# Rounds 3 to 7 of a recurrence kernel: w, k and r loaded in runs of steps and turned by VectorE in 32x32 squares

## The chip, the core and the metric

The kernel runs on one core of a Trainium2 chip. The core has five instruction streams that run side by side and wait for each other through semaphores: PE (TensorE, matrix products, which take their weights through a separate load, PEld), DVE (VectorE), ACT (ScalarE), POOL (GpSimd) and SP (SyncE, which here only issues DMAs). PE writes to PSUM, from where DVE or ACT copy results to SBUF. The metric is device time in microseconds (us) of one execution of the whole program, the median of three runs.

## What is computed

A recurrence over 768 steps for 4 batches and 8 heads of 48 columns, then a layer norm and a two-layer MLP with a residual, on rows of 8 x 48 = 384 columns. All in 32-bit floats.

```python
# r, k, v, w: (4, 8, 768, 48); u: (8, 48)
for t in range(S):
    kt, vt, rt, wt = (k[:, :, t], v[:, :, t], r[:, :, t], w[:, :, t])
    cur = np.einsum('bhd,bhe->bhde', u[None] * kt, vt)
    y[:, :, t] = np.einsum('bhd,bhde->bhe', rt, state + cur)
    state = wt[:, :, :, None] * state + np.einsum('bhd,bhe->bhde', kt, vt)
...
x = y as (4, 768, 384)
mu, var = mean and variance of x over its 384 columns
xn = (x - mu) / np.sqrt(var + 1e-06) * g_ln
out = x + np.maximum(xn @ w_ch1, 0.0) @ w_ch2     # 384 -> 1536 -> 384
```

## The kernel before

**Rounds and units.** The 4 x 768 steps are cut into 8 rounds of 384 steps, each of two units of four heads. Even rounds begin a batch. Round r's recurrence runs while the MLP of the round before fills PE's time; the loop variable `rnd` counts the round whose recurrence is on.

**The recurrence by levels.** Steps are handled in chunks of 64. The decay between two steps is built up by doubling, in six levels (`NLEV`): on level `lev`, `quads` multiplies, for all chunks of a unit, the r of the right half of each block of 2 x 2^lev steps with the k of its left half (`a_ps`, 96 small products for a round and level in the profile), `grow` then multiplies r and k by the decays (`tot`, products of w made by `totals`) so that they fit the next level (`rkT`, two instructions on DVE), and `keep` copies the right places of the products into the chunk matrix A (a copy under a mask on DVE). So each level is a chain: PE, DVE, PE. `ends`, `states`, `exchanged`, `own_outputs` and `outputs` carry the state from chunk to chunk and make the outputs (`kn_ps`, `kv`, `s`, `sx`, `y`, `x`).

**Turned inputs.** `quads` wants w, k and r with the head column on the partitions and the steps along the row. Two heads stand in the two halves of the 128 partitions (a pair, `pr`). Before the change `load` brings `nat[nm]`, 128 steps by heads of 64 columns of which 48 are filled, in three DMAs a tensor and unit (rows of 192 bytes), one round ahead; `turned` turns one pair of one unit with three TensorE transposes of 128x128 into a PSUM tile of the pool `ps_t` (two buffers), and ACT copies it to `rkT` or `wT`. Three tensors, two units and two pairs make 12 such calls, 36 transposes, in a round. `own_products` also reads the natural k and r, for the term of a step with itself (`rk`, `own`, `vo`).

**What fills PE.** `mlp` is a generator of 24 steps: 12 that make one 128-row part of the hidden layer each (`h_ps`, copied through ReLU by ACT), and 12 that add up outputs (`o_ps`, to which DVE adds x). Each step is three 32-bit products of 384 columns, which the profile shows as six matmuls. `fill(until, tasks)` spreads a level's list of tasks evenly among the MLP steps due by then (`UNTIL`). In level 3 the statistics and `norm` of the finished round make `xn` on DVE; in level 4 `turned_x` turns `xn` on PE (`xT_ps`) for the next MLP.

**Which level turns what.** With `first = 3` in `rnd` 2 and `first = 1` after that, level `first` turns w of both units of the next round, the next level k and r of its first unit, the one after that k and r of its second unit.

**Order.** PE, ACT, DVE and POOL, and DMAs issued through `SPO`, are held to the order of the program. DMAs issued through `SP` are placed in the queue by a scheduler; once placed, the queue is in order too. The tag `raw` has four buffers; before the change only the MLP's weights pass through them, in `rnd` 0 and 1.

**The start.** Round 0's w, k and r come in whole rows by `load_rows`, from SP and from ACT. ACT loads its function table for a first square root (`root`). `warm` issues products of a zero tile (`nought`, "idle" in the profile).

Of the kernel before, what the change touches and what calls it, by code (L numbers as in the profile page):

```python
# [9 lines left out]
F32 = mybir.dt.float32  # L10
# [4 lines left out]
AF = mybir.ActivationFunctionType  # L15
# [37 lines left out]
def kernel(  # L53
# [16 lines left out]
    SP = nc.sync  # L70

    B, H, S, D = r.shape
    P = 128
# [59 lines left out]
    def load_rows(nm, q, eng):  # L133

        b, f, g = units[q]
        src = {"w": w, "k": k, "r": r}[nm]
        eng.dma_start(
            out=flat(nm, q)[:, 0 : NH * TT * D].rearrange("p (h x) -> p h x", h=NH),
            in_=src[b, ts(g, NH), ds(f * RN, RN)].rearrange("h (p c) d -> p h (c d)", c=TT),
        )  # L140

    def load_v(q, eng=SP):
        vn[q] = p4.tile([P, TT, NH, D], F32, tag="v", name=f"v{q}")
        for c in range(TT):
            eng.dma_start(out=vn[q][:, c], in_=steps(v, q, c))
# [9 lines left out]
            )  # L155


    nought = const.tile([P, 1], F32, name="nought")
    DVE.memset(nought, 0.0)
    eps = const.tile([P, 1], F32, name="eps")  # L160
    DVE.memset(eps, 1e-6)
    load_rows("r", 0, ACT)

    ACT.activation(out=const.tile([P, 1], F32, name="root"), in_=eps, func=AF.Sqrt)
    for q in range(U):
        load_rows("w", q, SPO)
        load_rows("k", q, SPO)
    load_rows("r", 1, ACT)

    sel = const.tile([P, H // 2, 2], F32, name="sel")  # L170
    POOL.memset(sel, 0.0)
    for j in range(2):
        ACT.dma_start(
            out=sel[ds(HP * j, D), :, j], in_=u.rearrange("(r j) d -> j d r", j=2)[j]
        )
    g_sb = const.tile([P, KC], F32, name="g_sb")
    u_bc = const.tile([P, H, D], F32, name="u_bc")
    ident = const.tile([P, P], F32, name="ident")
    make_identity(nc, ident)
    for q in range(U):  # L180
        for nm in "wrk":
            POOL.memset(flat(nm, q)[:, NH * TT * D :], 0.0)
# [109 lines left out]
    def warm(n, tag="m"):  # L292

        while n > 0:
            m = min(n, RN // P)
            ps = (ps_m if tag == "m" else ps_t).tile([P, RN], F32, tag=tag, name="idle")
            PE.matmul(
                ps[:, 0 : m * P], nought.broadcast_to([P, P]), nought.broadcast_to([P, m * P]),
                start=True, stop=True,
            )  # L300
            n -= m


    st, carry = {}, {}

    def turned(q, nm, pr):
        a = st.setdefault(q, {})
        if pr == 0:
            if nm == "w":
                if q % U == 0:  # L310
                    st["w"] = p1.tile([P, U, W], F32, tag="w", name=f"wT{q // U}")
                a["w"] = st["w"][:, q % U]
            elif "rk" not in a:

                rk = a["rk"] = p4.tile([P, 2, W], F32, tag="rkT", name=f"rkT{q}")
                a["r"], a["k"] = rk[:, 0], rk[:, 1]
        ps = ps_t.tile([P, RN], F32, tag="t", name=f"{nm}_ps{q}_{pr}")
        if q < U:


            for c in range(TT):
                for j in (1, 0):
                    at = ((2 * pr + j) * TT + c) * D - HP * j
                    PE.transpose(
                        ps[0 : HP * (j + 1), ts(c, P)],
                        flat(nm, q)[:, ds(at, HP * (j + 1))], ident,
                    )
            (DVE.tensor_copy if q == 0 and pr else ACT.copy)(
                out=a[nm][:, ts(pr, RN)].rearrange("p (m c) -> p m c", c=TT),
                in_=ps.rearrange("p (c m) -> p m c", c=TT),  # L330
            )
            return
        for c in range(TT):
            PE.transpose(
                ps[:, ts(c, P)],
                nat[nm][q % 2][:, c, ts(pr, 2)].rearrange("p j d -> p (j d)"), ident,
            )
        ACT.copy(out=a[nm][:, ts(pr, RN)], in_=ps)
# [46 lines left out]
    def product_sums(q):  # L385
        b, f, g = units[q]
        a = st[q]
        ps = ps_t.tile([P, RN], F32, tag="t", name=f"own_ps{q}")
        for pr in pairs:
            for c in range(TT):  # L390
                PE.matmul(
                    ps[:, ts(pr * TT + c, 2)], a["ruk"][pr][:, ts(c, P)],
                    sel[:, NP * g + pr], start=True, stop=True,
                )
        o = a["own"] = p4.tile([P, TT, NH], F32, tag="own", name=f"own{q}")
        ACT.copy(
            out=o.rearrange("p c (r j) -> p r c j", j=2),
            in_=ps[:, 0 : 2 * NK].rearrange("p (r c j) -> p r c j", r=NP, j=2),
        )
# [145 lines left out]
    def own_outputs(q, tag="a"):  # L545

        y = ys[q] = banks(tag, f"y{q}")
        A = a_bufs[q // U % 2]
        for k_ in range(NK):
            pr, c = divmod(k_, TT)  # L550
            for i in range(2):
                for j in range(2):
                    rows = ds(C * (i ^ j), C)
                    PE.matmul(
                        y[j][ds(C * i, C), k_], A[rows, j, q % U, k_, :],
                        vx[q][rows, c, pr] if j else vn[q][rows, c, 2 * pr],
                        start=k_ == 0, stop=False, skip_group_check=True,
                    )

    def outputs(q):  # L560
        b, f, g = units[q]
        if q not in ys:
            own_outputs(q)
        a, y = st.pop(q), ys.pop(q)
        if g == 0:
            xs[b, f] = p2.tile([P, TT, H, D], F32, tag="x", name=f"x{b}_{f}")

        for k_ in range(NK):
            pr, c = divmod(k_, TT)
            for i in range(2):  # L570
                for j in range(2):
                    rows = ds(HP * (i ^ j), D)
                    if i:
                        R, s = a["rx"][rows, k_], a["sx"][rows, pr, c]
                    elif c:
                        R, s = a["r"][rows, ts(2 * k_, C)], a["s"][rows, pr, 2 * c - 1]
                    elif a["before"] is not None:
                        R, s = a["r"][rows, ts(2 * k_, C)], a["before"][rows, pr, 2 * TT - 1]
                    else:
                        continue  # L580
                    PE.matmul(
                        y[j][ds(C * i, C), k_], R, s,
                        start=False, stop=True, skip_group_check=True,
                    )
        for j in range(2):
            DVE.tensor_tensor(
                out=xs[b, f][:, :, ts(g, NH)]
                .rearrange("p c (r j) e -> p j r c e", j=2)[:, j],
                in0=y[j].rearrange("p (r c) e -> p r c e", r=NP),
                in1=a["vo"].rearrange("p c (r j) e -> p j r c e", j=2)[:, j], op=ALU.add,  # L590
            )
        del vn[q], vx[q]
# [117 lines left out]
    def each(f, *ranges):  # L710
        calls = [()]
        for r_ in ranges:
            calls = [c + (x,) for c in calls for x in r_]
        return [lambda c=c: f(*c) for c in calls]
# [37 lines left out]
    begin()  # L752
    begin()
    load(new[1], "k", SPO)
    SPO.dma_start(out=g_sb, in_=moe_g_ln.rearrange("(kc p) -> p kc", p=P))
    warm(3)
    grow(u1, 0)
    keep(0, 0)
    ahead = each(turned, new[:1], "wrk", pairs) + each(turned, new[1:], "wrk", pairs)
    for lev in range(1, NLEV):  # L760
        quads(u0, lev)
        if lev == 1:
            product_sums(u0)
        quads(u1, lev)
        run(ahead[2 * lev - 2 : 2 * lev] if lev < NLEV - 1 else [])
        if lev in (2, 3, 4):
            begin()
        if lev < NLEV - 1:
            warm(3)
        for which in ("rk",) if lev < NLEV - 1 else "kr":  # L770
            for q in (u0, u1):
                grow(q, lev, which)
        keep(0, lev)
# [13 lines left out]
    product_sums(u1)  # L787
    own_term(u1, POOL)
    own_outputs(u0)
    outputs(u0)  # L790
    exchanged(u1)
    begin()
    shifted()
    own_outputs(u1, "m")
    warm(2, "t")
    outputs(u1)
    moments(0)
    load(units_of(2)[0], "w", SPO)
# [23 lines left out]
    for rnd in range(1, NR + 1):  # L822
# [3 lines left out]
        for lev in range(NLEV):  # L826
# [37 lines left out]
                if lev in (4, 5):  # L864
                    own_term(now[lev - 4], POOL)
            if rnd == 2 and lev == 0:
                tasks += each(load_v, now) + each(load, new, "w")
            if rnd == 2 and lev == 2:
                for q in now:
                    take(DVE, q)  # L870
                    tasks += each(load, new[q % U :][:1], "kr")
            if rnd == 2 and lev in (3, 4):
                tasks += each(own_term, now[lev - 3 :][:1], [POOL])
            if rnd > 2 and lev < 2:
                tasks += each(load, new, ["w", "kr"][lev])
            first = 3 if rnd == 2 else 1
            if rnd > 1 and new and first <= lev < first + 3:
                m = lev - first
                tasks += each(turned, new[m - 1 : m], "kr", pairs) if m else each(
                    turned, new, "w", pairs  # L880
                )
            if rnd == 2:
                if lev == 0:
                    tasks += each(exchanged, old)
# [78 lines left out]
```

## Time and profile before

| | |
|---|---|
| median of three runs | 586.68 us (586.47 to 587.8) |
| the profiled execution | 586.47 us |
| its span, first to last instruction | 584.7 us |
| mean granted TensorE clock | 0.991 |
| `o_ps` matmuls | 576, 199.1 us busy |
| `h_ps` matmuls | 576, 198.9 us busy |
| `a_ps` matmuls | 4608, 78.7 us busy |
| `w_ps`, `k_ps`, `r_ps` transposes | 108 each, 273 ns at the median for one |
| ACT copies of these | 31 each, 0.48 us at the median |
| bytes moved | 36.52 MB, 62 GB/s over the span |
| `nat_w`, `nat_k`, `nat_r` loads | 42 each of 96 KB, 3.2, 3.0 and 2.8 us from issue to landing |

Busy time counts a stretch once where instructions of a group overlap. Matmuls are pipelined, so the length of one is more than what it adds to the end. An arrow in the views names what a wait ended on.

### The profile page before, as it was taken

What the parts mean: (1) busy time and instruction counts of PE and PEld (TensorE: products, weight loads), DVE (VectorE), ACT (ScalarE), POOL (GpSimd) and SP (SyncE); (2) the same over time, 40 slices, a digit from 0 to 9 for tenths busy, and PEclk for the clock granted to TensorE, in tenths of its full rate; (3) what the DMA queues carried; (4) which work ended last, traced back from release to release, by engine and by line L of the source; (5) the groups of instructions that cost most, each with busy time, mean ns of one, the idle gap of its engine ahead of it and who ended that gap; (6) DMA issues with size and microseconds to landing.
All of it is one profiled execution on the core that took longest, in us unless ns stands there. A gap on an engine that the chain in (4) does not pass through costs nothing.

```text
span 584.7 us, 19058 instructions
## 1 busy us (share of the span) xinstructions
PE 571.7 (98%) x8560; PEld 383.3 (66%) x8560; DVE 273.5 (47%) x576; ACT 193.9 (33%) x423; POOL 91.5 (16%) x124
## 2 busy tenths in 40 slices
PE   9999989999999999999999999999999999999997
PEld 6776755666666666666666666667666666666554
DVE  5869899677264634343462543336254531130000
ACT  3657686402442124211432114312331015202200
POOL 7140011104340026000620008000320000000000
PEclk9979899999999999999999999999999999999999
DMA  9937885037314311340205302021000000000000
GB/s 232 212 91 142 198 240 129 9 84 137 61 25 97 77 30 28 63 95 16 57 3 93 65 29 43 2 61 31 15 2 2 16 28 2 2 15 27 0 15 27
DMA packets 114192, 36.52 MB, mean 62 GB/s; under 512 B 104768, under 2 KB 111040, under 8 KB 114112
## 3 DMA queue, kind: packets, MB, share of 16 engines
q1 hardware_dynamic: 112640, 34.72, 26.7%
q8 instruction: 67, 1.10, 0.8%
q10 hardware_dynamic: 1472, 0.59, 0.4%
q14 instruction: 13, 0.11, 0.1%
HBM read 28.51 MB, written 4.72 MB: 57 GB/s over the span
## 4 chain that ended last, share of the span: by engine, by line
PE 91%; ACT 4%; DVE 2%; issue 1%; POOL 1%; DVEq 0%; ACTq 0%; POOLq 0%
PE o_ps L49 32%; PE h_ps L49 30%; PE a_ps L49 11%; PE y L49 4%; PE kv L49 2%; PE k_ps L49 2%; PE w_ps L49 2%; PE kn_ps L49 2%; PE r_ps L49 2%; PE xT_ps L49 1%; ACT rest L49 1%; PE idle L49 1%; PE own_ps L49 1%; ACT rkT L49 1%; DVE w_sb L49 1%
## 5 line engine op out<-in xcount | busy, mean ns | idle before, releaser
L49 PE MATMUL o_ps<-w_sb,h 128*128 128x384 f32 x576 | 199.1, 490 | 0.8 <-ACT h L49 0.8
L49 PE MATMUL h_ps<-xT,w_sb 128*128 128x384 f32 x576 | 198.9, 493 | 0.0
L49 PEld LDWEIGHTS h_ps<-xT,w_sb 128*128 128x128 f32 x576 | 105.7, 191 | 63.0 <-issue 0.9
L49 PEld LDWEIGHTS o_ps<-w_sb,h 128*128 128x128 f32 x576 | 104.4, 190 | 61.8 <-ACT h L49 1.4
L49 ACT ACTIVATE h<-h_ps 128x384 f32<-128x384 f32 x96 | 46.9, 489 | 144.9 <-PE h_ps L49 144.8
L49 DVE TENSOR_TENSOR rkT<-rkT,tot 128x768 f32<-128x768 f32 (+1 forms) x96 | 75.9, 831 | 40.4 <-issue 26.0
L49 PEld LDWEIGHTS a_ps<-rkT 48*64 48x64 f32 x4608 | 73.3, 136 | 21.6 <-issue 15.7
L49 PE MATMUL a_ps<-rkT 48*64 48x32 f32 x4608 | 78.7, 221 | 0.6 <-issue 0.5
L49 DVE TENSOR_TENSOR o<-o_ps,x 128x384 f32<-128x384 f32 x24 | 13.4, 557 | 121.9 <-PE o_ps L49 121.8
L49 POOL TENSOR_TENSOR vo<-v,own 128x576 f32<-128x576 f32 x16 | 19.4, 1213 | 288.5 <-DVE own L49 251.3
L49 DVE SCALAR_TENSOR_TENSOR s<-s,decay,kv 128x48 f32<-128x48 f32 x160 | 29.3, 259 | 33.9 <-PE kv L49 33.9
L49 DVE TENSOR_TENSOR x<-y,vo 128x288 f32<-128x288 f32 x32 | 13.1, 452 | 53.9 <-PE y L49 53.9
L49 DVE COPY_PREDICATED A<-mask,a_ps 128x768 f32<-128x768 int8 x32 | 38.3, 1198 | 0.0
L49 ACT COPY rkT<-k_ps 128x384 f32<-128x384 f32 x31 | 13.8, 478 | 55.5 <-PE k_ps L49 55.5
L49 ACT ACTIVATE xT<-xT_ps,g_sb 128x384 f32<-128x384 f32 x24 | 13.6, 580 | 54.0 <-PE xT_ps L49 54.0
L49 ACT COPY rkT<-r_ps 128x384 f32<-128x384 f32 x31 | 14.1, 479 | 24.1 <-PE r_ps L49 24.1
L49 DVE TENSOR_SCALAR w_sb<-w_sb 128x384 f32<-128x384 f32 (+1 forms) x48 | 19.6, 409 | 0.8
L49 ACT COPY wT<-w_ps 128x384 f32<-128x384 f32 x31 | 14.0, 479 | 17.0 <-PE w_ps L49 17.0
L49 ACT ACTIVATE rstd<-mv,eps 128x3 f32<-128x3 f32 x8 | 2.4, 296 | 49.5 <-DVE mv L49 49.4
L49 DVE TENSOR_REDUCE own<-rk 128x12 f32<-128x576 f32 x12 | 9.0, 750 | 20.7 <-POOL rk L49 20.6
L49 DVE TENSOR_TENSOR rkT<-rkT,wT 128x768 f32<-128x768 f32 x16 | 17.8, 1146 | 0.9 <-PE a_ps L49 0.8
L49 PE MATMUL r_ps<-ident,nat_r 128*128 128x128 f32 x108 | 16.1, 277 | 2.1 <-ACT rkT L49 2.1
(76 smaller groups left out, 517.6 us busy)
## 6 DMA issues: line engine op xcount, KB each, us to landing
raw<-in_moe_w_ch_dram SPq DMA_DIRECT2D x24, 384.0 KB, 4.5
v<-in_v_dram SPq DMA_DIRECT2D x48, 96.0 KB, 3.0
out_dram<-o SPq DMA_DIRECT2D x24, 192.0 KB, 1.9
nat_w<-in_w_dram SPq DMA_DIRECT2D x42, 96.0 KB, 3.2
nat_r<-in_r_dram SPq DMA_DIRECT2D x42, 96.0 KB, 2.8
nat_k<-in_k_dram SPq DMA_DIRECT2D x42, 96.0 KB, 3.0
vx<-v SPq DMA_DIRECT2D x28, 72.0 KB, 2.9
nat_w<-in_w_dram SPq DMA_DIRECT2D x2, 288.0 KB, 4.9
```

The costliest lines, as they stand in the source:

```text
L49: return lambda *args, **kw: self.tc.keep_in_program_order(f(*args, **kw))
```

## The change

In `rnd` 2 to 6, w, k and r of the next round are no longer turned by TensorE. `stage` loads one pair of one unit into a tile with the tag `raw`: partition 64j + 32e + x of it holds the run of steps 12x to 12x + 11 of head j of the pair, from column 32e on, 560 numbers that are contiguous in memory. So each 32x32 square of the tile (32 runs by 32 columns, at one step of the run) turned in place gives 32 columns on the partitions by 32 steps. `squares` does the twelve squares of a tile in one DVE transpose, and writes them with a stride of 12 steps. Columns 48 to 63 then hold numbers of the next step in place of zeros; no product reads them into a result. The last pair of the last unit would read past the tensor, so it is loaded in smaller pieces, after a memset. The natural w isn't loaded for these rounds; the natural k and r still are. `stage` runs one level ahead of `squares`.

At the start, the two `load_rows` of r, `sel` and `g_sb` are issued from ACT ahead of its first function table, `product_sums(u0)` goes behind the turns of level 1 in place of an idle product, and an idle product stands before `outputs(u0)` in place of one before `outputs(u1)`.

```diff
+    SQ = 32
+    NS = RN // SQ
+    ROW = (NS - 1) * D + SQ
+    staged = {}
+
+    def stage(q, nm, pr, eng=SP):
+        b, f, g = units[q]
+        src = {"w": w, "k": k, "r": r}[nm]
+        t = p4.tile([P, WC, 2], F32, tag="raw", name=f"{nm}_runs{q}_{pr}")
+        t = staged[q, nm, pr] = t.rearrange("p n two -> p (n two)")[:, 0 : NS * D]
+        for j in range(2):
+            first = src.offset + ((b * H + g * NH + 2 * pr + j) * S + f * RN) * D
+            if (q, pr, j) == (NU - 1, NP - 1, 1):
+
+                POOL.memset(t[P - SQ :, NS * D - SQ :], 0.0)
+                both = [(e, 1, ROW - e * (ROW - NS * D + SQ)) for e in range(2)]
+            else:
+                both = [(0, 2, ROW)]
+            for e, many, n in both:
+                eng.dma_start(
+                    out=t[ds(HP * j + SQ * e, SQ * many), 0:n],
+                    in_=bass.AP(
+                        tensor=src.tensor, offset=first + SQ * e,
+                        ap=[[SQ, many], [NS * D, SQ], [1, n]],
+                    ),
+                )
...
-    load_rows("r", 0, ACT)
-
-    ACT.activation(out=const.tile([P, 1], F32, name="root"), in_=eps, func=AF.Sqrt)
     for q in range(U):
         load_rows("w", q, SPO)
+        load_rows("r", q, ACT)
         load_rows("k", q, SPO)
-    load_rows("r", 1, ACT)
...
     g_sb = const.tile([P, KC], F32, name="g_sb")
+    ACT.dma_start(out=g_sb, in_=moe_g_ln.rearrange("(kc p) -> p kc", p=P))
...
+    ACT.activation(out=const.tile([P, 1], F32, name="root"), in_=eps, func=AF.Sqrt)
...
+    def squares(q, nm, pr):
+        a = st[q] if pr else turned_to(q, nm)
+        DVE.transpose(
+            out=a[nm][:, ts(pr, RN)].rearrange("p (t s) -> p s t", s=NS),
+            in_=staged.pop((q, nm, pr)).rearrange("p (s d) -> p s d", s=NS)[..., 0:SQ],
+        )
...
     load(new[1], "k", SPO)
-    SPO.dma_start(out=g_sb, in_=moe_g_ln.rearrange("(kc p) -> p kc", p=P))
...
     for lev in range(1, NLEV):
         quads(u0, lev)
-        if lev == 1:
-            product_sums(u0)
         quads(u1, lev)
         run(ahead[2 * lev - 2 : 2 * lev] if lev < NLEV - 1 else [])
         if lev in (2, 3, 4):
             begin()
-        if lev < NLEV - 1:
+        if lev == 1:
+            product_sums(u0)
+        elif lev < NLEV - 1:
             warm(3)
...
     own_outputs(u0)
+    warm(3, "t")
     outputs(u0)
     exchanged(u1)
     begin()
     shifted()
     own_outputs(u1, "m")
-    warm(2, "t")
     outputs(u1)
...
             if rnd == 2 and lev == 0:
-                tasks += each(load_v, now) + each(load, new, "w")
+                tasks += each(load_v, now)
...
-            if rnd > 2 and lev < 2:
-                tasks += each(load, new, ["w", "kr"][lev])
+            if rnd > 2 and lev == 1:
+                tasks += each(load, new, ["kr"])
             first = 3 if rnd == 2 else 1
-            if rnd > 1 and new and first <= lev < first + 3:
+            if rnd > 1 and new and first - 1 <= lev < first + 3:
                 m = lev - first
-                tasks += each(turned, new[m - 1 : m], "kr", pairs) if m else each(
-                    turned, new, "w", pairs
-                )
+                turns = [(new, "w"), (new[:1], "kr"), (new[1:], "kr")]
+                if m >= 0:
+                    tasks += each(squares, *turns[m], pairs)
+                if m < 2:
+                    tasks += each(stage, *turns[m + 1], pairs)
```

`turned_to` is the part of `turned` that makes the tiles `wT` and `rkT`, now a function of its own.

More of the change, by code (lines that the diff above doesn't have):

```diff
@@ L155, in load_vx @@
             )
[L158 to L161, printed above, removed]
-    load_rows("r", 0, ACT)
-    ACT.activation(out=const.tile([P, 1], F32, name="root"), in_=eps, func=AF.Sqrt)
     for q in range(U):
         load_rows("w", q, SPO)
+        load_rows("r", q, ACT)
         load_rows("k", q, SPO)
-    load_rows("r", 1, ACT)
     sel = const.tile([P, H // 2, 2], F32, name="sel")
@@ L179 @@
     make_identity(nc, ident)
+    nought = const.tile([P, 1], F32, name="nought")
+    DVE.memset(nought, 0.0)
+    eps = const.tile([P, 1], F32, name="eps")
+    DVE.memset(eps, 1e-6)
+    ACT.activation(out=const.tile([P, 1], F32, name="root"), in_=eps, func=AF.Sqrt)
     for q in range(U):
@@ L304, with turned_to @@
     st, carry = {}, {}
-    def turned(q, nm, pr):
[L307 to L316, printed above, removed]
+    def turned_to(q, nm):
+        a = st.setdefault(q, {})
+        if nm == "w":
+            if q % U == 0:
+                st["w"] = p1.tile([P, U, W], F32, tag="w", name=f"wT{q // U}")
+            a["w"] = st["w"][:, q % U]
+        elif "rk" not in a:
+            rk = a["rk"] = p4.tile([P, 2, W], F32, tag="rkT", name=f"rkT{q}")
+            a["r"], a["k"] = rk[:, 0], rk[:, 1]
+        return a
+    def squares(q, nm, pr):
[4 more added lines that the diff above has]
+        )
+    def turned(q, nm, pr):
+        a = st[q] if pr else turned_to(q, nm)
         ps = ps_t.tile([P, RN], F32, tag="t", name=f"{nm}_ps{q}_{pr}")
```

## The prediction

> **What bounds the kernel now.** I read the page first: TensorE is busy for 98% of the span.
>
> ```profile
> span 584.7 us, 19058 instructions
> PE 571.7 (98%) x8560; PEld 383.3 (66%) x8560; DVE 273.5 (47%) x576; ACT 193.9 (33%) x423; POOL 91.5 (16%) x124
> ```
>
> Second, busy time by stretch. The first three stretches are levels 1, 2 and 3 of round 5, in which the inputs of round 6 are turned; the last three are the same levels of round 7, which has no inputs left to turn. Columns: stretch, length, then busy time of PE, weight load, DVE, ACT, POOL, then the granted clock, the DMA share and GB/s.
>
> ```profile
> 299.98:314.30 14.32, 14.32 (x231) 9.54 (x225) 6.42 (x17) 4.32 (x10) 0.00 (x0) 1.00 0.31 58
> 314.30:326.78 12.48, 12.48 (x225) 8.55 (x227) 4.09 (x6) 1.82 (x4) 0.00 (x0) 1.00 0.51 104
> 326.78:335.58 8.80, 8.80 (x131) 6.05 (x132) 5.74 (x13) 2.02 (x5) 0.00 (x0) 1.00 0.13 25
> 435.61:448.61 13.00, 13.00 (x218) 8.37 (x213) 6.43 (x17) 2.83 (x6) 0.00 (x0) 1.00 0.01 3
> 448.61:459.82 11.21, 11.21 (x212) 7.38 (x215) 4.09 (x6) 0.00 (x0) 0.00 (x0) 1.00 0.06 20
> 459.82:467.36 7.54, 7.54 (x119) 4.83 (x122) 5.73 (x13) 0.30 (x1) 0.00 (x0) 1.00 0.01 2
> ```
>
> PE fills both kinds of level without a gap, and DVE is about half idle. So here a turn taken off PE is time taken off the end, as long as DVE can carry it without making PE wait.
>
> Third, the timeline of DVE in level 3 of round 5, then of round 3, each followed by the PE row that waits for it: the turning of the normalized rows (`xT_ps`), the first thing PE does after level 4's 96 small products. Columns: start, length, engine, instruction.
>
> ```profile
> 329.48 0.96 DVE L49 COPY_PREDICATED A<-mask,a_ps 128x768 f32<-128x768 int8 x1
> 330.35 1.48 DVE L49 BATCH_NORM_STATS2 stats<-x 128x6 f32<-128x384 f32 x3
> 331.74 0.30 DVE L49 BATCH_NORM_AGGREGATE mv<-stats 128x2 f32<-128x6 f32 x3
> 332.63 0.17 DVE L49 RECIPROCAL rstd<-rstd 128x3 f32<-128x3 f32 x1 [0.60 <-ACT rstd L49]
> 332.85 1.26 DVE L49 TENSOR_SCALAR xn<-x,mv,rstd 128x384 f32<-128x384 f32 x3
> 337.05 0.55 PE L49 MATMUL xT_ps<-ident,xn 128*128 128x128 f32 x3
> ...
> 199.69 0.54 DVE L49 TENSOR_TENSOR o<-o_ps,x 128x384 f32<-128x384 f32 x1
> 201.04 1.26 DVE L49 TENSOR_SCALAR xn<-x,mv,rstd 128x384 f32<-128x384 f32 x3
> 203.36 0.87 PE L49 MATMUL xT_ps<-ident,xn 128*128 128x128 f32 x6
> ```
>
> Spare time there: `xn` ends at 334.1 and is wanted at 337.1, 3.0 us; in round 3 it is 202.3 against 203.4, 1.1 us. Fourth, ACT's start and the clock of the early stretches:
>
> ```profile
> 1.34 1.28 ACT L49 ACT_TABLE_LOAD   x1 [1.34 <-PEq L947]
> 4.97 0.33 ACTq L49 DMA_DIRECT2D sel<-in_u_dram  x1
> 5.59 0.48 ACT L49 COPY wT<-w_ps 128x384 f32<-128x384 f32 x1 [2.75 <-PE w_ps L49]
> ...
> 30.00:33.00 3.00, 1.63 (x8) 0.45 (x7) 1.41 (x2) 2.19 (x5) 0.00 (x0) 0.77 0.77 239
> 33.00:36.00 3.00, 3.00 (x99) 2.94 (x99) 0.77 (x2) 0.00 (x0) 0.00 (x0) 0.50 0.55 143
> ```
>
> **PE's turns go.** Each of rounds 2 to 6 turns 36 blocks for the next round: 180 PE turns and 60 ACT copies of 0.48 us. Their price on the path is the difference of the six stretches: 14.32 - 13.00 = 1.32, 12.48 - 11.21 = 1.27, 8.80 - 7.54 = 1.26, together 3.85 us a round, or 107 ns a turn, well under the 273 ns that one shows by itself. Rounds 3 to 6: 4 x 3.85 = 15.4 us. Round 2 turns in levels 3 to 5. By the chain, level 5 there lasts 10.06 us from the end of its small products (152.44) to the `kv` products (162.50), of which three MLP steps are 6.03 and twelve `kn` turns 1.3; the remaining 2.7 us for twelve turns holds waits for ACT copies that free the two PSUM buffers. With 1.27 for each of the other two levels, and 2.5 for this one (the `kn` turns keep some of the waits), round 2 gives 5.0 us (between 3.85, no wait saved, and 5.6). Sum: -20.4 us. ACT's 60 x 0.48 = 29 us are worth nothing more; ACT is a third busy.
>
> **DVE's squares come.** 60 transposes of 128x384 f32, four in each of three levels, behind the level's masked copy. The trace has no such instruction. Nearest rows, 384 columns in f32: 407 ns (`w_sb`, SBUF to SBUF) and 557 ns (`o`, from PSUM); `xn` runs three in 1.26 us, 0.42 each. The far bounds: 0.97 us, the row of twice the width, if each element takes two passes; and 2.18 us, if each of the twelve squares costs what a 128x24 instruction does (12 x 0.182). I take 0.46 us, since the work is one SBUF read and one write of 384 columns. Levels 1 and 2: DVE stands idle after the masked copy for 6.6 and 5.2 us (305.7 to 312.2, 318.0 to 323.1), so 1.84 us of squares is hidden. Level 3 has less cover: the built order puts the squares between the statistics and `xn`, and PE arrives 1.26 us sooner. Rounds 4 to 6: aggregation ends at 332.04; + 4 x 0.46 + 0.17 + 1.26 and small gaps = 335.3, wanted at 337.1 - 1.26 = 335.8: no wait, and none up to 0.58 us a square. Round 3: the order is three squares, the `o` addition, the fourth square, then `xn`: 199.69 + 1.84 + 0.5 + 0.2 + 1.2 = 203.4, wanted at 203.4 - 1.26 = 202.1: PE waits 1.3 us. Queued behind the squares are also the additions that free `o_ps` banks; PE needs such a bank two groups later, so they have over 4 us.
>
> By the Trainium skill, page VectorE: DVE Perf Modes, section The three transpose paths, a 128x128 bf16 transpose takes 311 ns on VectorE against 390 ns on TensorE; three of these would be 0.93 us for our tile, an estimate, and the sum below would end near 574. The same page's 390 ns is not what this trace shows TensorE to lose, 107 ns. This rule speaks against the change more than the rows do.
>
> **Transfers.** 60 tiles are loaded in 123 DMAs, 64 runs of 2,240 bytes each as a rule (143 KB); the 30 loads of `nat_w` for these rounds go, the natural k and r stay for the own-step products. SP issues one in 0.5 us (three `nat_k` in 1.49), so (123 - 30) x 0.5 = 46 us more over five rounds of SP time that is mostly waiting. Landing: 3.0 us for 96 KB, 4.5 us for 384 KB. Each tile waits for one of the four `raw` buffers, so for the square before it. Level 3's runs are the latest: SP first waits for v of the next unit and its copy (316.0 + 1.27, less 1.3), then issues eight from 317 on, ending near 321, landed by 325.7; the first square wants its tile at 332.0 - 2.6 = 329.4. 3.7 us to spare, cost 0. POOL gains three tiny memsets; the round 7 products behind them are wanted 25 us later.
>
> **The start.** In the changed order ACT issues r0, r1, both `sel` and `g_sb` before the function table. `sel`'s second load waited until 4.97, for the first DMA's landing, whose counter it reuses; now `g_sb` is the one that waits: 4.97 + 0.50 (its issue row on SP) + 1.28 + 0.20 (`root`) = 6.95, so the first copy moves from 5.59 by 1.4 us, and with it r's turns on PE, which need that PSUM buffer. `product_sums(u0)` moves behind level 1's turns, and that level's idle product (0.65 us in the chain) goes; DVE waited 0.71 us at 18.9 for the small products that stood behind those sums, and DVE is the busier engine until 31 us, so 0.7 us comes back. The idle product before `outputs` only changes place. Net +0.7 us. Bounds: the half-clock stretch after the 1.37 us gap at 30.1 costs (2.72 - 1.53) + (2.91 - 1.4) = 2.7 us now; it may vanish or come twice, so -2.0 to +3.4.
>
> The skill's page TensorE: Matmul & The Clock Gate, Part 1, says that an idle window of about 3.4 us halves the clock; this trace has the drop to 0.50 after a shorter gap, and by the page's window neither the 1.4 us at 6 us nor the gap at 30 would do it.
>
> **Sum.** The profiled execution took 586.47 us (span 584.7, 1.8 around it), 0.2 under the median of 586.68. 586.5 - 20.4 + 1.3 + 0.7 = 568.1; I say 568.
>
> **Rivals.** (1) The squares cost about 0.97 us. Then `xn` is late in every round: 1.3 + 4 x 0.51 = 3.3 in round 3, and 4 x 0.97 - 2.34 = 1.5 in each of rounds 4 to 6, 7.9 in all in place of 1.3: 574.7. For it: the squares are turned in blocks and written with a stride of 48 bytes. Against: the strided `rkT` products show no extra time. (2) Slower: the squares cost 2.18 us. The gain without stalls, 19.7 us, is used up when 0.1 + 16 x (s - 0.46) reaches it, at s = 1.7 us. At 2.18, four a level are 8.7 us, over the idle time of levels 1 and 2, so level 3 starts late too: some 7 us in each of rounds 3 to 6 and 3 in round 2, 586.5 - 19.7 + 31 = 598. Against it: no DVE row of 384 columns is over 0.56 us. (3) The runs come late: SP's queue is in order, and a `v` load or output that waits ahead of the runs holds them. DVE then waits at a square with `xn` behind it. It costs nothing up to 3.7 us of lateness; at 6 us, 2.3 to 3 us in each of four rounds: 579. (4) The removed turns are not on the path: excluded by the six stretches, unless a hidden wait takes their place.
>
> **Chances.** Forecast 0.66 (its own range 565 to 571.5), rival (1) 0.18, (2) 0.07, (3) 0.06, (4) 0.03. The range goes from 565 (the half-clock stretch gone) to 577 (rival (1) with a second such stretch). A change under 0.2% (1.2 us) can't be told from none. Faster: 0.66 + 0.18 + most of (3) = 0.88; within 0.2%: 0.03; slower: 0.09.
>
> **What would show it.** Right: levels 1 to 3 of rounds 3 to 6 last 13.0, 11.2 and 7.5 us; a DVE transpose row near 0.46 us; a gap of about 1.3 us before `xT_ps` in round 3 only; the first ACT copy near 7.0 us. Wrong: a transpose over 0.58 us with gaps before every `xT_ps`, DVE waits on the run tiles, or a lower clock after 40 us.

## The result and the profile after

The changed kernel took 744.75 us at the median of four runs (742.75 to 746.18); the kernel before took 586.64 us beside it. The ratio is 1.2687, with a 95% interval of 1.2653 to 1.2722: 158 us slower, where 18 us faster was forecast. The profiled execution has a span of 742.8 us.

First the page of the changed kernel: span, the busy time of PE, the transposes of r on DVE (busy time and mean ns, then the idle time before them and what ended most of it).

```profile
span 742.8 us, 18836 instructions
...
PE 575.3 (77%) x8378; PEld 379.4 (51%) x8378; DVE 321.5 (43%) x636; ACT 168.9 (23%) x363; POOL 95.1 (13%) x127
...
L49 DVE STREAM_TRANSPOSE rkT<-r_runs 128x384 f32<-128x384 f32 x20 | 17.0, 848 | 98.7 <-DMA r_runs<-in_r_dram 98.7
```

PE was busy for 98% of the span and is now at 77%. DVE stood idle for 98.7 us in front of the squares of r, and all of it ended with the landing of a run tile; k's row has 76.4 us more, 74.6 of it for the same reason. The waits of PE that are new (total, times, longest) lead back to DVE and make 153.9 us:

```profile
PE xT_ps L49 <- DVE xn L49: 89.3, 4, 24.9
PE a_ps L49 <- DVE rkT L49: 46.9, 7, 21.2
PE kn_ps L49 <- DVE rkT L49: 17.7, 1, 17.7
```

Now levels 1 and 3 of round 5, as the prediction showed them, and the stretch from there to the first `xT_ps` (busy time by stretch: length, PE, weight load, DVE, ACT, POOL, granted clock, DMA share, GB/s):

```profile
406.96:420.07 13.11, 13.11 (x227) 8.48 (x218) 9.16 (x21) 2.83 (x6) 0.00 (x0) 1.00 0.26 55
...
431.32:443.80 12.48, 8.54 (x154) 5.77 (x154) 4.71 (x8) 0.00 (x0) 0.00 (x0) 0.96 0.23 61
443.80:470.09 26.29, 1.79 (x68) 1.66 (x65) 6.22 (x14) 0.30 (x1) 0.00 (x0) 0.50 0.21 63
```

Level 1 is as short as forecast (13.0 us), and so is level 2 (11.25 us, 11.2 forecast): the turns did go. Level 3 is not (7.5 us forecast), and after its small products PE does 1.8 us of work in 26 us, at half the clock. DVE and SP in that stretch (timeline: start, length, engine, instruction, idle time before it; on SP the length is that of the issuing):

```profile
451.03 0.84 DVE L49 STREAM_TRANSPOSE rkT<-k_runs 128x384 f32<-128x384 f32 x1 [4.92 <-DMA k_runs<-in_k_dram]
456.80 0.85 DVE L49 STREAM_TRANSPOSE rkT<-k_runs 128x384 f32<-128x384 f32 x1 [4.93 <-DMA k_runs<-in_k_dram]
462.72 0.85 DVE L49 STREAM_TRANSPOSE rkT<-r_runs 128x384 f32<-128x384 f32 x1 [5.07 <-DMA r_runs<-in_r_dram]
468.65 0.84 DVE L49 STREAM_TRANSPOSE rkT<-r_runs 128x384 f32<-128x384 f32 x1 [5.09 <-DMA r_runs<-in_r_dram]
...
469.56 1.26 DVE L49 TENSOR_SCALAR xn<-x,mv,rstd 128x384 f32<-128x384 f32 x3
```

```profile
442.35 2.50 SPq L164 DMA_DIRECT2D k_runs<-in_k_dram  x4
444.89 11.12 SPq L164 DMA_DIRECT2D r_runs<-in_r_dram  x4
456.11 2.69 SPq L709 DMA_DIRECT2D out_dram<-o  x1
```

The four squares stand in front of `xn` and come every 5.8 to 5.9 us, one tile of two loads at a time, so about 2.9 us a load. SP issues four loads in 11.1 us, 2.8 us each, where it issued four in 2.5 us just before: its queue now moves on at the pace of the transfers, as a full one would. What stands behind is held too: the output at 456.11 takes 2.7 us to issue. While that lasts the DMA engines are almost idle (busy time by stretch, columns as above, of the time in which SP issues at that pace):

```profile
444.89:456.01 11.12, 0.70 (x28) 0.57 (x23) 2.06 (x7) 0.30 (x1) 0.00 (x0) 0.50 0.14 51
```

A share of 0.14 is little more than 2 of 16 engines (0.125). The access pattern of a load is `[[SQ, 2], [NS * D, SQ], [1, 560]]`: its outermost dimension is 2. So the theory is (an estimate from these rows): such a load runs on two DMA engines, and 143 KB at 51 GB/s take 2.8 us. A round has 24 of them, 24 x 2.8 = 67 us, all the 67.8 us that a round took before, but they may only start level by level and are wanted one level later. The rivals: SP's in-order queue alone (another queue would help), and DVE's order or its squares (the transfers would matter little).

The first `xT_ps` of rounds 3 to 7 starts at 203.36, 269.23, 337.05, 404.86 and 470.86 us before, and at 279.63, 374.46, 470.09, 560.80 and 629.41 after. So the 158 us were lost as 76.3 up to round 3, then 29.0, 27.8, 22.9 and 2.6 us.

### The profile page after: what moved, and what is told of

Read it like the earlier page. It is cut to its first block, busy times and chain, and to the rows that moved or that the text cites. A ratio compares the mean times of both kernels' runs of the same rounds, so it can differ in the third digit from the quotient of the medians.

```text
span 742.8 us, 18836 instructions
## 1 busy us (share of the span) xinstructions
PE 575.3 (77%) x8378; PEld 379.4 (51%) x8378; DVE 321.5 (43%) x636; ACT 168.9 (23%) x363; POOL 95.1 (13%) x127
## 4 chain that ended last, share of the span: by engine, by line
PE 47%; DMA 22%; issue 10%; SPq 8%; DVE 7%; ACT 3%; POOL 2%; DVEq 0%; POOLq 0%; ACTq 0%
PE h_ps L49 17%; DMA r_runs<-in_r_dram 16%; PE o_ps L49 16%; PE a_ps L49 5%; DMA k_runs<-in_k_dram 4%; SPq L164 4%; SPq L125 3%; DVE rkT L49 3%; PE y L49 2%; DMA nat_r<-in_r_dram 2%; POOL rk L49 1%; PE kv L49 1%; DVE A L49 1%; PE xT_ps L49 1%; PE kn_ps L49 1%
## 5 line engine op out<-in xcount | busy, mean ns | idle before, releaser
L49 PE MATMUL o_ps<-w_sb,h 128*128 128x384 f32 x576 | 205.2, 506 | 1.0 <-ACT h L49 1.0
L49 PEld LDWEIGHTS o_ps<-w_sb,h 128*128 128x128 f32 x576 | 109.3, 197 | 69.5 <-issue 5.9
L49 PE MATMUL a_ps<-rkT 48*64 48x32 f32 x4608 | 83.5, 227 | 48.3 <-DVE rkT L49 46.9
L49 PEld LDWEIGHTS a_ps<-rkT 48*64 48x64 f32 x4608 | 77.7, 143 | 69.3 <-DVE rkT L49 51.4
L49 PE MATMUL xT_ps<-ident,xn 128*128 128x128 f32 x72 | 15.5, 322 | 89.8 <-DVE xn L49 89.3
L49 PEld LDWEIGHTS xT_ps<-ident,xn 128*128 128x128 f32 x72 | 10.3, 157 | 98.3 <-DVE xn L49 91.8
L49 DVE STREAM_TRANSPOSE rkT<-r_runs 128x384 f32<-128x384 f32 x20 | 17.0, 848 | 98.7 <-DMA r_runs<-in_r_dram 98.7
L49 DVE STREAM_TRANSPOSE rkT<-k_runs 128x384 f32<-128x384 f32 x20 | 17.1, 853 | 76.4 <-DMA k_runs<-in_k_dram 74.6
L49 PE MATMUL kn_ps<-ident,rkT 128*128 128x128 f32 x96 | 14.8, 291 | 18.6 <-DVE rkT L49 17.7
L49 PEld LDWEIGHTS kn_ps<-ident,rkT 128*128 128x128 f32 x96 | 11.8, 148 | 24.5 <-DVE rkT L49 18.3
```

The source lines that it names most:

```text
L49: return lambda *args, **kw: self.tc.keep_in_program_order(f(*args, **kw))
```

## The experiments

**The loads and the squares by themselves.** The first probe timed 64 rows of 2,240 bytes in patterns that differ in how the 64 rows are split, `[[32, 2], [576, 32]]` to `[[4, 16], [576, 4]]` and plain `[[576, 64]]`, each followed by a small DVE copy that waits for it, and DVE transposes.

> This kernel computes none of the reference: it only times loads and DVE transposes one by one. Theory A (a load is spread over as many DMA engines as its outermost dimension has entries, here 2): with 64 rows of 2,240 bytes each, the form 2 x 32 lands some 2.9 us of transfer after its start, 4 x 16 in half of the transfer time, 8 x 8 in a quarter, 16 x 4 and plain 64 rows in an eighth, so about 5, 3.4, 2.7, 2.4, 2.4 us from issue to use; six loads in a row take 17 us in the form 2 x 32 and under 4 us as plain rows. Theory B (runs that overlap in memory, or runs of 2,240 bytes, are slow to read): 4 x 16, 8 x 8 and 16 x 4, which overlap more, are as slow as 2 x 32, and plain 64 rows alone is fast, or none is. DVE: if the stride of 12 in the write makes a transpose 0.85 us, the dense one takes 0.46 us and the strided copy 0.85; if the transpose itself costs two passes, dense and strided both take 0.85, the half tile 0.45 and the strided copy 0.4 to 0.5.

Timeline of DVE in the probe; in the names "two" is the outermost dimension 2, and so on. Each copy stands behind one of the same form, so its idle time and its 0.16 us are the time between two landings.

```profile
8.94 0.16 DVE L20 COPY one_two<-one_two 64x8 f32<-64x8 f32 x1 [2.84 <-DMA one_two<-in_w_dram]
...
21.06 0.16 DVE L20 COPY one_eight<-one_eight 64x8 f32<-64x8 f32 x1 [0.81 <-DMA one_eight<-in_w_dram]
...
23.87 0.16 DVE L20 COPY one_plain<-one_plain 64x8 f32<-64x8 f32 x1 [0.40 <-DMA one_plain<-in_w_dram]
...
50.12 3.48 DVE L20 STREAM_TRANSPOSE y<-x 128x384 f32<-128x384 f32 x4
53.46 2.37 DVE L20 STREAM_TRANSPOSE dense<-x 128x384 f32<-128x384 f32 x4
```

The same bytes land 3.0 us apart with an outermost dimension of 2, 1.7 with 4, 0.97 with 8 and 0.56 with 64: up to 8 the time falls nearly as the dimension grows (those with 16 were all but in when DVE came to them). The third load of the first form landed 4.6 us behind the second, with loads of the next form issued by then. Six in a row landed every 3.17 us at the mean in the first form (28.01 to 43.88 us) and every 0.61 us in the plain one (46.27 to 49.33). Theory B is out: the forms with 4 and 8 overlap more in memory and are faster. A square in the kernel's form takes 0.85 us at the mean (four in 3.48), one with a dense output 0.57 us (four in 2.37). A plain copy into the same stride took 0.49 us (four in 2.07), so the stride costs extra only in the transpose, which neither of the two expected cases had.

**Loads of 32 rows.** The changed kernel, each load cut in two with 32 rows outermost.

```diff
-            else:
-                both = [(0, 2, ROW)]
-            for e, many, n in both:
+            for e in range(2):
+                n = ROW - e * (ROW - NS * D + SQ) if last else ROW
                 eng.dma_start(
-                    out=t[ds(HP * j + SQ * e, SQ * many), 0:n],
+                    out=t[ds(HP * j + SQ * e, SQ), 0:n],
...
-                        ap=[[SQ, many], [NS * D, SQ], [1, n]],
+                        ap=[[NS * D, SQ], [1, n]],
```

> The changed kernel with each load cut in two, so that its outermost dimension has 32 rows in place of 2; bytes, runs and tiles are the same, loads are 243 in place of 123. Theory A: loads land in 3 us, DVE no longer waits for runs but for a few us, and the time is 586.6 - 20.4 for the turns, + 6.1 for xn that is late behind squares of 0.85 us, + 0 to 5 for SP, which issues 16 loads a level in 8 us: 572 to 578. Theory B (the volume or the shape of the runs): within 10 us of 745. Theory C (squares of 0.85 us are the cost): also near 745, with DVE busy where it now waits.

It took 579.2 us (577.6 to 582.9, seven runs) against 585.96 us before: ratio 0.9894, 0.9858 to 0.9929. With the same bytes in twice as many loads 165.6 us are gone, and the kernel is 1.1% faster than before: the outermost dimension was the loss. The loads of k now land 1.9 us after their issue at the median. But 579 is just over theory A's range, and not the 568 of the forecast. A part of what was left shows in the waits of PE:

```profile
PE a_ps L49 <- DVE s L49: 2.2, 1, 2.2
PE xT_ps L49 <- DVE xn L49: 2.1, 1, 2.1
```

and in DVE's order in level 3 of round 3 of the same kernel (timeline):

```profile
200.94 1.54 DVE L49 STREAM_TRANSPOSE rkT<-k_runs 128x384 f32<-128x384 f32 x2
...
203.48 0.81 DVE L49 STREAM_TRANSPOSE rkT<-r_runs 128x384 f32<-128x384 f32 x1
...
204.36 1.26 DVE L49 TENSOR_SCALAR xn<-x,mv,rstd 128x384 f32<-128x384 f32 x3
```

The squares stand before `xn`, as the prediction had read from the built order, and PE waits for `xn`. Apart from the start, the new gaps of PE of over 1 us lie in rounds 2 and 3, where squares stand before `own_sums` and the chain of `s` too. The waits cost more than their length, since PE's granted clock was lower behind them. By stretch (columns as above), in this kernel:

```profile
150.00:205.00 55.00, 48.24 (x852) 31.84 (x850) 38.52 (x75) 10.38 (x23) 13.30 (x12) 0.91 0.51 126
```

The kernel before has a granted clock of 1.00 from 150 to 201.9 us. Here it was 0.50 from 162 to 164, 172 to 178 and 206 to 208 us, each time behind a wait of PE (0.94, 2.25 and 2.09 us).

**The start alone.** The kernel before with nothing but the changed start.

> The kernel before with nothing but the changed start (order of the first loads, function table, product_sums, idle products). By the prediction +0.7 us, 587.3. By the trace of the changed kernel, whose small products before the first MLP begin at 46.9 against 47.7, -0.7 us: 585.9.

It took 585.84 us against 585.96: ratio 0.9999, 0.9974 to 1.0024. The start is worth nothing that can be told.

**The loads alone, read by nobody.** The kernel before, with the two-engine loads issued as in the changed kernel, and TensorE's turns (and so the loads of the natural w) kept.

```diff
+            if rnd > 1 and new and first - 1 <= lev < first + 2:
+                turns = [(new, "w"), (new[:1], "kr"), (new[1:], "kr")]
+                tasks += each(stage, *turns[lev - first + 1], pairs)
```

> The kernel before, TensorE turns and all, with the run loads of the change (outermost dimension 2) issued as well and read by nobody. If the cost is that DVE waits for the runs at a square, with PE behind it, the time stays under 600: loads of 2.8 us each hold SP's queue, and only v, natural k, r, w and outputs behind them can be late. If the loads cost by themselves (queue, memory, engines), it goes most of the way to 745.

It took 802.19 us, ratio 1.368 (1.3622 to 1.3738). The first case, under 600 us, is out, and the second is exceeded: nothing reads these tiles, and still the kernel lost more than the changed one. A row of SP's timeline in this run, and the busy time by stretch (columns as above) while it issues these five loads:

```profile
452.78 11.28 SPq L161 DMA_DIRECT2D k_runs<-in_k_dram  x5
```

```profile
452.78:464.06 11.28, 0.00 (x0) 0.00 (x0) 0.00 (x0) 0.00 (x0) 0.00 (x0) 0.50 0.13 49
```

For 11 us no engine works at all, with the DMA share at 0.13. `nat_w`, `nat_k`, `v` and the outputs stand behind the runs: the longest single waits for them were 99.3 us (POOL, for `nat_k`) and 62.7 us (DVE, for an output to leave). PE itself waited 56.3 us for `nat_k`, and 142.4 us for DVE (`rkT` and `o`). So DVE's wait at the squares is only one way in which the transfers cost time; the loads and stores behind them are another.

**Is it the queue or the engines?** A second probe sent two-engine loads over one and two queues, then plain loads behind them, and turned tiles into outputs of different strides.

> This kernel computes none of the reference. First part: six loads in the changed kernel's form (outermost dimension 2, 32 rows of 2,240 B in each half), once all on SP's queue and once alternately on SP's and ScalarE's queue, then six in the plain form (64 rows outermost). Theory A (the two DMA engines that an outermost dimension of 2 reaches are the limit): the six take the same time on two queues as on one, 18 to 20 us at the 3.17 us each of the first probe, and the plain six 3 to 4 us. Rival B (a queue serves one such load at a time and the engines are free): on two queues 9 to 11 us. Second part: a 192 KB load with 128 rows outermost, issued behind two loads of the changed form on one queue: theory A' (the engines work through their own lists) lands it no later than the second of the two plus 0.6 us, about 8 us after the first issue; rival: it overtakes on the 14 other engines, and only the pieces on the first two engines hold it. Third part: transposes of 128 x 384 in f32 by VectorE whose output stands 1, 2, 4, 8, 12, 13 and 16 elements apart: if it is a stride of 12 that costs 0.27 us over the dense 0.58 us, the strides 2 to 16 should take 0.85 us each; if it is the number of bytes that a row spans, the time grows with the stride.

ScalarE issued its three at once, so they ran beside SP's first six. Busy time by stretch of the probe (DVE, POOL, clock, DMA share, GB/s): the two-engine loads of both queues, then a piece of the time in which the plain ones were issued.

```profile
8.00:29.00 21.00, 0.90 (x6) 0.00 (x0) 1.00 0.13 51
...
31.00:33.50 2.50, 0.00 (x0) 0.00 (x0) 1.00 0.88 134
```

With two queues at work the share stays at 0.13 and the rate at 51 GB/s, those of SP's queue alone in the changed kernel (0.14, 51): theory A, the engines are the limit. The plain loads then took up most of the engines (0.88 from 31 to 33.5 us), but the first of them was complete only at 41.55 us, behind the last two-engine load at 40.75: so the plain loads overtake, except for pieces that come last. That fits pieces on the two shared engines, which the trace doesn't name. So these two-engine loads delayed the completion of the plain loads that followed. The load of 192 KB with 128 rows outermost was complete at 50.81 us, 12.8 us after the first issue of its part, where theory A' had about 8; the last plain load had landed at 44.69, and two more loads of 2.8 us behind it make 50.3, an estimate. When those two landed doesn't show, since DVE looked at them last. The Trainium skill, page DMA: Bandwidth & Descriptors, has a rule on the number of engines in its section Rules for kernel authors: it follows from the slowest dimension that isn't 1, so a small outermost one confines the whole DMA to at most as many engines. The runs agree (shares of 0.13 to 0.14; 3.0, 1.7 and 0.97 us for 2, 4 and 8).

The strides, in stretches of three transposes each (DVE's busy time, clock, DMA share, GB/s; the count has those that touch the stretch too); shown are those with output elements 2 and 4 apart:

```profile
53.56:55.29 1.73, 1.66 (x5) 1.00 0.00 0
55.29:57.72 2.43, 2.36 (x5) 1.00 0.00 0
```

A third of the length is one: 0.58 us for 2, as for 1, and 0.81 us for 4; 8, 12, 13 and 16 took 0.81 to 0.83 us. It is a step between 8 and 16 bytes, which neither expectation had.

**The loads on ScalarE's queue.** In the changed kernel `stage` got ACT in place of SP.

> The changed kernel, with the loads of runs in the same form (outermost dimension 2) but issued by ScalarE instead of SyncE. Theory A (two DMA engines are the limit, at 3 us a load, 24 loads of a level pair against 65 us of a round, and all other transfers need those two engines too): still far above the time before, 700 to 760 us, since the squares wait for the same loads and nat k, r, w and v still need the two engines. Rival B (the loss is SyncE's in-order queue, behind which the other loads stand): below 640 us.

778.21 us, ratio 1.3271 (1.3236 to 1.3306), 18 us over theory A's upper end. ACT's own work now stands behind the full queue: from 447.74 us on it issues two loads in 8.46 us, and then comes the next copy of `h` (timeline of ACT):

```profile
456.30 0.49 ACT L49 ACTIVATE h<-h_ps 128x384 f32<-128x384 f32 x1 [11.26 <-DMA k_runs<-in_k_dram]
```

and PE waited 55 us in all for `h`, against 1.0 us in the changed kernel. So the time by itself doesn't settle rival B: a gain on SP's queue could hide behind ACT's loss. DVE's wait for the runs does (total, times, longest):

```profile
DVE rkT L49 <- DMA r_runs<-in_r_dram: 95.2, 20, 5.7
```

With the runs off SP's queue it is nearly what it was, 98.7 us. With the second probe's two queues at the rate of one, rival B is out.

**The order on DVE.** To the loads of 32 rows this adds that the squares go behind `xn` in level 3, and behind the first `own_sums` in level 5 of round 2.

```diff
-                if m >= 0:
-                    tasks += each(squares, *turns[m], pairs)
+                late_squares = each(squares, *turns[m], pairs) if m >= 0 else []
+                if lev < (5 if rnd == 2 else 3):
+                    tasks += late_squares
...
                     tasks += each(norm, [rnd - 1])
+                    tasks += late_squares if new else []
...
                     tasks += each(own_products, new[1:], [POOL])
+                    tasks += late_squares if rnd == 2 else []
                     tasks += each(own_sums, new[1:]) + each(own_term, new[1:], [POOL])
```

> The loads of 32 rows of the run before (579.2 us), with VectorE's squares placed behind the normalized rows (xn) in level 3 of rounds 3 to 6 and behind the first own-term sums in round 2. Theory (the rest of the loss is VectorE's order in rounds 2 and 3: squares stand ahead of xn, sums and the decay's chain, 12 us lost between 130 and 205 us): 568 to 573 us. Rival (it is the SyncE queue, 16 issues a level of about 0.45 us each in front of nat r and nat k, or the extra 0.39 us that a square takes over my estimate): no change, 577 to 582 us.

568.18 us (565.51 to 569.48, six runs) against 585.93: ratio 0.9681, 0.9655 to 0.9706. This is the fastest version, ahead of both kernels. Its page, and level 3 of round 5 on DVE with PE's `xT_ps` behind it:

```profile
PE 550.1 (97%) x8378; PEld 364.4 (65%) x8378; DVE 315.6 (56%) x636; ACT 168.3 (30%) x363; POOL 92.6 (16%) x127
```

```profile
317.86 1.26 DVE L49 TENSOR_SCALAR xn<-x,mv,rstd 128x384 f32<-128x384 f32 x3
319.03 1.54 DVE L49 STREAM_TRANSPOSE rkT<-k_runs 128x384 f32<-128x384 f32 x2
...
321.03 0.55 PE L49 MATMUL xT_ps<-ident,xn 128*128 128x128 f32 x3
```

`xn` is ready 1.9 us before PE wants it, and the squares lie beside PE's work. The order alone is worth 579.2 - 568.2 = 11 us, in waits and in the clock behind them (from 130 to 210 us it was 1.00 here and 0.91 with the loads of 32 rows alone).

**Squares only from round 3 on.** The same, but round 2 keeps TensorE's turns for the inputs of round 3.

> As the run before, but with TensorE's turns and the plain loads kept for the inputs of round 3, so that loads of runs and squares begin with the inputs of round 4 (48 squares instead of 60). Theory (the loss stands in round 2 alone, where VectorE and SyncE carry the products, the copies and the squares at once): round 2 as before, then 3.0 to 3.85 us gained in each of four rounds: 586 - 12 to 15.4 = 570.5 to 574 us. Rival (the loss is spread over all rounds): 577 us or more.

571.82 us, ratio 0.9742 (0.9715 to 0.977): 14.1 us under the kernel before, in the range of the first theory. But the squares stand behind `xn` here too, so the run doesn't tell whether the loss stood in round 2 alone. It is 571.82 - 568.18 = 3.6 us slower than the version with all squares, which is what round 2's turns were worth (the six runs of each spread over 4 us).

## Why the prediction was wrong, point by point

**The step that failed** is "**Transfers**", with the words "Landing: 3.0 us for 96 KB, 4.5 us for 384 KB" and "3.7 us to spare, cost 0". It took the time of a run load from rows of loads that put 128 partitions outermost, and asked only for bytes, for the number of runs and for SP's time to issue. It did not look at the outermost dimension of the new pattern, 2. By the runs such a load holds two engines for 2.8 us, eight in a row 22 us, where SP's issuing was costed at 4 us. So the runs of level 3 came late by far more than the spare time, and the sign of being wrong that the prediction named, DVE waits on the run tiles, came true. The term costed at 0 measured 165.6 us (744.75 against 579.2, the same bytes in 32-row loads). Rival (3) named the right wait, with DVE at a square and `xn` behind it, but put its cause in the order of SP's queue and its size at 579 us; the transfers themselves were not doubted. The queue matters, as the unread loads show, but as one thing that passes the delay on to other transfers.

**PE's turns** were right for rounds 4 to 6, and put too high for rounds 2 and 3. From one first `xT_ps` to the next, with the order mended, rounds 4 to 6 took 62.02, 63.96 and 63.96 us, before 65.87, 67.82 and 67.81: 3.85 to 3.86 us less in each, against 3.85 predicted. Up to the first `xT_ps` of round 3 the gain was 203.36 - 195.05 = 8.3 us in the two profiled executions. But 2.6 us of it stand already at the first `xT_ps` of all, before any square (49.9 against 47.3 us), where the clock was 0.50 from 32 to 38 us in the one execution and 1.00 from 14 to 47 us in the other: luck of that execution, since the start alone measured nothing. The other 5.7 us are rounds 2 and 3, where the steps had 5.0 + 3.85 less 1.3, 7.55. By the medians of the last two runs round 2's turns were worth 3.6 us, not the 5.0 of the sum and just under the lower bound of 3.85. How the rest of the shortfall came about is open.

**The squares** were mis-sized: 0.46 us taken, 0.85 us measured for one alone (0.73 in a row, four in 2.94 us). That is near the bound of 0.97 us, rival (1), and the reason named there holds: in the transpose the stride costs 0.25 us, and the dense form is at 0.58. In levels 1 and 2 it is hidden, as said. In level 3 it is not, with the squares before `xn`: with the loads of 32 rows PE waited 2.1 us in round 3 (1.3 predicted) and, which the prediction didn't have, stood 9.8 us behind the mended order by then (204.89 against 195.05, of which 1.2 us are from the start); round 4 took 64.27 us, 2.2 more, with the clock at 0.50 at its head, and rounds 5 and 6 took 64.31 us, 0.35 more. That the rest was DVE's order, not SP's 16 issues a level, is shown by the run that changed the order alone. Which of the moved squares was worth how much was not tried.

**The start** was put at +0.7 us and measured nothing: 585.84 against 585.96. Its mechanism was right as far as the first ACT copy goes, which came at 6.80 us (near 7.0 forecast); that delay cost nothing that can be told.

**The sum.** 568 us was reached (568.18) only by the version that has neither the two-engine loads nor the squares ahead of `xn`. That it meets the number so closely is in part luck: rounds 2 and 3 gave 5.7 us where 8.85 were put in for their turns, and the losses of 1.3 us (`xn` in round 3) and 0.7 us (start) were not there. It holds as the worth of the turns with everything else hidden, which the changed kernel didn't give.

## What to carry to other kernels

Before a transfer is costed by the rows of others, compare the outermost dimension of its access pattern with theirs: with equal bytes and run lengths, 2 in place of 64 made a load five times as long here, and the loads and stores behind it were late too. A DMA share near 2/16 while a queue takes microseconds for each issue is the sign of it. Work that is moved to an idle engine belongs behind that engine's part of the critical chain: the same squares cost 11 us more ahead of it than behind it.

## What the runs showed of the hardware that was not expected

- Six plain loads issued behind two-engine loads kept the DMA engines 88% busy from 31 to 33.5 us, and yet the first was complete only at 41.55 us, after the last two-engine load.
- VectorE's transpose of 128x384 f32 takes 0.58 us with outputs up to 8 bytes apart and 0.81 to 0.83 us from 16 bytes on, up to 64.
- Loads that nobody reads cost the kernel 216 us (802.19 against 585.96).
